# Another order of the stages in the first ten steps of a fused attention and feed-forward kernel

## The chip, the cores and the metric

The kernel runs on one core of one Trainium2 chip. The metric is the device time of one execution in microseconds. Before the change the median of three runs is 623.97 us (623.69 to 624.47). The times in the rows below come from one further execution, which the hardware profiler recorded.

## The reference

The reference computes attention over 2 batches of 8 heads with 768 positions of 64 numbers. A position sees the first 4 positions (the sinks) and the last 128 up to itself. The result, 1536 rows of 512, goes through two feed-forward nets:

```python
scores = np.where(keep, q @ k.T / 8, -1e9)        # keep = sink or 0 <= rel < 128
a = np.exp(scores - scores.max(-1, keepdims=True))
x = (a / (a.sum(-1, keepdims=True) + 1e-9)) @ v   # -> (1536, 512)
x = ((x @ w_a) * (x @ w_b)) @ w_out               # d_ff 1536
x = np.maximum(x @ w_in, 0)
y = (x * x) @ w_out2                              # d_ff 2048
```

## The kernel before

**Groups and steps.** Attention is cut into 24 groups: per batch six blocks of 128 query rows, per block two groups of four heads. Group g belongs to block g // 2. Blocks 0 and 6 are the first of a batch and have no earlier block, so their groups (0, 1, 12, 13) have no sinks and no selections. `attention_fast` runs a loop of 27 steps. Step g issues one stage each for several groups at once: a lag of -2 beside a stage's name in the lists `ORDER` and `AT_FIRST` means that step g does this stage for group g - 2. PE, DVE, ACT and POOL issue their instructions strictly in the order in which the lists name them; each waits in line for what its next instruction needs. `AT_FIRST` holds for the steps below `EARLY`, `ORDER` for the others.

**The stages of a group**, with their engine and line:
- `scores0`, `scores1` (PE, L243): scores of two heads each, into two PSUM tiles `sc`. They can be overwritten as soon as the maxima have read them.
- `soft0`, `soft1` (DVE, L259 and L262): a predicated copy, then mask and row maximum. Together they are called the maxima here.
- `exp0`, `exp1` (ACT, L270): exponentials and their sums, one step later.
- `rec` (DVE, L275 and L276): the reciprocals of the sums. `norm` (DVE, L283), `normA` (ACT, L290) and `normP` (POOL, L295) multiply one, one and two heads by them. `sp` (POOL, L305 to L307) does it for the sinks' columns and splits them into two parts.
- `pst` (PE, L337) and `st` (ACT, L343): the sinks' columns transposed and copied. `ptp` (PE, L313) and `th` (ACT, L317): the four heads transposed and copied. `lu` (POOL, L328 and L330): two selections, the lower and the upper triangle.
- `x0`, `x1` (PE, L362, from step 10 on L376 in two halves) and `xs` (PE, L392): the products with the values and with the sinks' values. `xh` (ACT, L400) and `xl` (DVE, L403): the result as a high and a low part.
- `warm`: matmuls of zeros (L414) in the steps up to 9, their number by `WARM`.
- Beside attention the weights of the first net are decoded, one piece per step of `DECODE` (4, 8, 10, 11, ...): `abs` on ACT (L589), `ts` on DVE in the same step (L593, L594), `stt` and `stt2` on DVE one step later (L597, L600), `cast` on ACT (L605) and `lo` on DVE (L607) two steps later. From step 11 on `fill` gives PE twelve matmuls of the first net per step (L720), and `fu` (ACT) and `fm` (DVE, L737) read their result in the next step.

**Queues.** SP issues the loads, in program order as the trace has it: block 0 in halves of two head pairs, then block 1 whole (`load_kq(1)`), the values, blocks further on and the weights. The sinks' values of a batch are loaded into `vsr` and split by `sink_split` at the end of the steps in `VS`: a copy on ACT (L220), and a subtraction of 32 x 512 numbers (L221) that waits for it. From step 10 on (`WIDE`) two PSUM banks fewer are at hand for `bank`, and POOL writes a `mark` (L382) between `x0` and `x1`, which `x1` waits for.

After step 26 PE alone has a written order; the feed-forward nets follow as one long row of 128x512 matmuls.

Of the kernel before, what the change touches and what calls it, by code (L numbers as in the profile page):

```python
# [10 lines left out]
F32 = mybir.dt.float32  # L11
# [18 lines left out]
ORDER = [  # L30
    ("exp0", -1), ("exp1", -1), ("fm", 0), ("pst", -2), ("rec", -1), ("st", -2), ("fu", 0), ("scores0", 0),
    ("x0", -3), ("scores1", 0), ("x1", -3), ("xs", -3), ("abs", 0), ("xh", -3), ("ptp", -2), ("th", -2), ("cast", -2), ("soft0", 0), ("soft1", 0), ("sp", -1),
    ("norm", -1), ("warm", 0), ("fill", 0), ("normA", -1), ("normP", -1), ("xl", -3), ("stt", -1),
    ("lo", -2), ("ts", 0), ("lu", -2), ("stt2", -1)]
AT_FIRST = [x for x in ORDER if x[0] not in ("rec", "warm")]
AT_FIRST.insert(AT_FIRST.index(("soft1", 0)) + 1, ("rec", -1))
AT_FIRST.insert(AT_FIRST.index(("ptp", -2)), ("warm", 0))
EARLY = 4
DECODE = [4, 8, 10, 11, 12, 13, 14, 15, 18, 19, 20]
WIDE = 10  # L40
VS = (3, 12)
FLAG = 22
SPARED = range(10, 18)
PINNED = 3
WARM0 = 14
WARM = {0: 2, 1: 4, 2: 6, 3: 8, 4: 9, 5: 6, 6: 6, 7: 6, 8: 6, 9: 6}
NQ, NV, NEX, NTH, NLU, NSP = 3, 5, 3, 2, 2, 2
T = 512
SW = P + SK
# [107 lines left out]
def attention_fast(tc, ctx, c, cp, tp, q, k, v, vs_in, xh, xl, beside):  # L157


    nc = tc.nc  # L160
# [21 lines left out]
    pns, ths, sps, sts, lus, xs = ({} for _ in range(6))  # L182
# [6 lines left out]
    def load_kq(n, part=slice(0, H // 2)):  # L189
        if n >= B * NB:  # L190
            return
        if n not in queries:
            queries[n] = p2.tile([P, H // 2, P], F32, name="queries", tag="queries", bufs=NQ)
        b, i = divmod(n, NB)
        nc.sync.dma_start(keys[:, part, i], k[b, i, :, part])
        nc.sync.dma_start(queries[n][:, part], q[b, i, :, part])

    def load_v(n):
        if n >= B * NB:
            return  # L200
        vals[n] = p2.tile([P, H, D], F32, name="values", tag="values", bufs=NV)
        nc.sync.dma_start(vals[n], v[n // NB, n % NB])

    with tc.high_priority(offset=1000):
        load_kq(0, slice(0, 2))
        load_kq(0, slice(2, 4))
    load_kq(1)
    load_v(0)


# [1 line left out]
    vs = p1.tile([96, B, H // 2, P], F32R, name="vs")  # L212
    vsr = {}

    def sink_load(b):
        vsr[b] = p1.tile([96, H // 2, P], F32, name="vsr", tag="vsr")
        nc.sync.dma_start(vsr[b], vs_in[:, b])

    def sink_split(b):
        nc.scalar.copy(vs[:, b], vsr[b])  # L220
        nc.gpsimd.tensor_sub(vs[64:96, b], vsr[b][64:96], vs[64:96, b].bitcast(F32))  # L221

    def half(t, r):
        return t[r * D:(r + 1) * D]
# [22 lines left out]
    def maxima(g, pp):  # L247

        b, i, m = groups[g]
        if pp == 0:  # L250
            pns[g] = (p2.tile([P, GH, SW], F32, name="ex", tag="ex", bufs=NEX),
                      p2.tile([P, GH], F32, name="ss", tag="ss", bufs=NEX),
                      p2.tile([P, GH], F32, name="nb", tag="nb", bufs=NEX))
        ex, ss, nb = pns[g]
        w, at = P if i == 0 else SW, PREV
        sc = scs[pp]
        if i > 0:
            other = sc[:, :, 0:2 * (PREV + SW)].rearrange("q r (u s) -> q r u s", u=2)[:, :, ::-1, 0:HK]
            nc.vector.copy_predicated(sc[:, :, at:at + P].rearrange("q r (u s) -> q r u s", u=2),  # L259
                                      c.pick.unsqueeze(1).to_broadcast([P, 2, 2, HK]), other)  # L260
        for h in range(2 * pp, 2 * pp + 2):
            nc.vector.tensor_tensor_reduce(  # L262
                out=ex[:, h, 0:w], in0=sc[:, h % 2, at:at + w], in1=c.m[min(i, 2)][:, 0:w], scale=-0.125,
                scalar=3.0e38, op0=ALU.add, op1=ALU.min, accum_out=nb[:, h:h + 1])

    def exps(g, pp):
        ex, ss, nb = pns[g]
        w = P if groups[g][1] == 0 else SW
        for h in range(2 * pp, 2 * pp + 2):
            nc.scalar.activation(ex[:, h, 0:w], ex[:, h, 0:w], AF.Exp, bias=nb[:, h:h + 1], scale=-1.0,  # L270
                                 accum_out=ss[:, h:h + 1])
# [80 lines left out]
    def values(g, turn):  # L352
        b, i, m = groups[g]
        apart = now[0] >= WIDE
        if apart and now[0] < N:
            return turned_values(g, turn)
        if turn == 0:
            return
        x = xs[g] = ps_x[0].tile([P, 2, T], F32, name="x", tag="x")[:, :, 0:P] if apart else bank("x")[:, 0:2]
        for j, probs_t in enumerate(lus.pop(g)):  # L360
            for h in range(GH):
                nc.tensor.matmul(half(x, h % 2)[:, h // 2], lhsT=vals[g // 2 - j][:, GH * m + h], rhs=probs_t[:, h],  # L362
                                 start=j == 0 and (apart or h < 2), stop=False, skip_group_check=True)
# [44 lines left out]
    def warm(n):  # L408

        if n == 0:  # L410
            return
        ps = bank("psw").rearrange("p h t -> p (h t)")[:, 0:2 * P]
        for _ in range(n):
            nc.tensor.matmul(ps, lhsT=beside.zero, rhs=beside.zero[:, 0:1].to_broadcast([P, 2 * P]), start=True,  # L414
                             stop=True)

    stages = dict(scores0=lambda g: scores(g, 0), scores1=lambda g: scores(g, 1), ptp=probs, th=probs_copy, lu=probs_select, soft0=lambda g: maxima(g, 0),
                  soft1=lambda g: maxima(g, 1), exp0=lambda g: exps(g, 0), exp1=lambda g: exps(g, 1), rec=reciprocal,
                  sp=sinks, pst=sinks_turn, st=sinks_copy, x0=lambda g: values(g, 0), x1=lambda g: values(g, 1), xs=sinks_values, xh=x_high, xl=x_low,
                  norm=normalize, normA=normalize_a, normP=normalize_p)  # L420
    now, ps_x = [0], []
    warm(WARM0)
    for g in range(N + 3):
        now[0] = g
        if g == WIDE:
            wide.close()
            ps_x[:] = [beside.stack.enter_context(tc.tile_pool(name="ps_x", bufs=1, space=PSUM, side="right"))]
            beside.lend(ps_t, "t1")
        elif g == N:
            ended.close()  # L430
            beside.open()
        if g % 2 == 0:
            load_kq(g // 2 + 2)
            load_v(g // 2 + 1)
        if g == 0:
            sink_load(0)
            later_masks(tc, cp, tp, c)
        elif g == FLAG:
            flag(tc, cp, c)
        beside.fetch(g)  # L440
        for name, lag in AT_FIRST if g < EARLY else ORDER:
            if name == "warm":
                warm(WARM.get(g, 0))
            elif name in stages:
                if 0 <= g + lag < N:
                    stages[name](g + lag)
            else:
                beside.stage(name, g + lag)
        if g in VS:
            sink_split(VS.index(g))  # L450
            if g == VS[0]:
                sink_load(1)
# [679 lines left out]
def sliding_window_moe_kernel(ctx, tc, q, k, v, vs, span, w_a, w_b, w_out, w_in2, w_out2, out):  # L1132
# [51 lines left out]
    def attend_any(ctx, beside):  # L1184
        attention_any(tc, c, q, k, v, xh, xl)
        beside.open()

    run(lambda ctx, beside: attention_fast(tc, ctx, c, cp, tp, q, k, v, vs, xh, xl, beside))
    slow = nc.values_load(c.slow[0:1, 0:1], min_val=0, max_val=1,
                          skip_runtime_bounds_check_because="the flag is 0 or 1")  # L1190
# [70 lines left out]
```

## Time and profile before

| | us |
|---|---|
| median of three runs | 623.97 |
| the profiled execution | 624.48 |
| its span, first to last instruction | 622.8 |
| PE busy in it | 608.0 (98%) |
| DVE busy | 480.4 (77%) |
| ACT busy | 303.5 (49%) |
| POOL busy | 64.8 (10%) |

POOL's work lies in the first 124 us, those of attention. A matmul's busy time is modelled, so whether PE is at its pace is read better from the starts of its instructions than from the share.

### The profile page before, as it was taken

The numbers are of one execution on the slowest core, as the hardware profiler recorded it, in microseconds if no ns is written. First come the engines' busy times: TensorE is split into PE (matmuls) and PEld (weight loads), VectorE is DVE, ScalarE is ACT, GpSimd is POOL, SyncE is SP. The second block draws the span as 40 slices with busy tenths as digits, with TensorE's granted clock in tenths as the row PEclk, the third lists the DMA queues.
The fourth block names the chain that finished last, engine by engine and source line by source line (L and its number), as shares of the span: only waits on it lengthen the run. The fifth ranks groups of instructions, "written<-read, shape, count | busy, mean of one in ns | idle before, by whom it ended". The sixth has DMA issues, their size and how long they took to land.

```text
span 622.8 us, 9656 instructions
## 1 busy us (share of the span) xinstructions
PE 608.0 (98%) x3525; PEld 494.4 (79%) x3525; DVE 480.4 (77%) x1079; ACT 303.5 (49%) x688; POOL 64.8 (10%) x157
## 2 busy tenths in 40 slices
PE   7989999999999999999999999999999999999995
PEld 4667778888888888888888888888888888888884
DVE  6889989369999948858869999977796779834352
ACT  5888887434744434434443554564453445232220
POOL 5665355400000000000000000000000000000000
PEclk9999999999999999999999999999999999999998
DMA  8934423012123313212302013232022202000032
GB/s 260 280 115 148 154 69 103 3 34 73 62 103 115 122 34 102 68 34 68 101 35 101 2 34 102 67 132 82 27 100 67 74 29 68 0 1 0 2 115 94
DMA packets 22041, 49.55 MB, mean 80 GB/s; under 512 B 2080, under 2 KB 8736, under 8 KB 21984
## 3 DMA queue, kind: packets, MB, share of 16 engines
q1 hardware_dynamic: 21696, 48.70, 24.5%
q8 instruction: 30, 0.49, 0.3%
q14 instruction: 27, 0.22, 0.1%
q10 hardware_dynamic: 288, 0.13, 0.1%
HBM read 45.68 MB, written 3.15 MB: 78 GB/s over the span
## 4 chain that ended last, share of the span: by engine, by line


## 5 line engine op out<-in xcount | busy, mean ns | idle before, releaser
L720 PE MATMUL psa<-xh,wh 128*128 128x512 f32 x224 | 88.6, 396 | 0.1
L720 PE MATMUL psa<-xh,wl 128*128 128x512 f32 x224 | 87.4, 390 | 0.0
L720 PE MATMUL psa<-xl,wh 128*128 128x512 f32 x224 | 87.3, 390 | 0.0
L980 PE MATMUL acc<-wh,gh 128*128 128x512 f32 x192 | 74.7, 389 | 0.0
L980 PE MATMUL acc<-wh,gl 128*128 128x512 f32 x192 | 74.7, 389 | 0.0
L980 PE MATMUL acc<-wl,gh 128*128 128x512 f32 x192 | 74.7, 389 | 0.0
L607 DVE TENSOR_TENSOR wl<-wtmp,wh 128x512 fp32r<-128x512 f32 x68 | 48.5, 717 | 17.2 <-ACT wh L605 17.0
L605 ACT CAST wh<-wtmp 128x512 fp32r<-128x512 f32 x68 | 42.3, 622 | 36.8 <-PE acc L980 10.0
L73 ACT CAST gh<-ks 128x512 fp32r<-128x512 f32 x48 | 29.7, 622 | 52.5 <-PE acc L980 52.5
L589 ACT ACTIVATE wtmp<-wraw 128x512 f32<-128x512 f32 x68 | 45.5, 673 | 19.3 <-DVE wl L74 12.7
L980 PE MATMUL acc<-gh,wh 128*128 128x512 f32 x136 | 52.9, 389 | 0.0
L980 PE MATMUL acc<-gl,wh 128*128 128x512 f32 x136 | 52.9, 389 | 0.0
L980 PE MATMUL acc<-gh,wl 128*128 128x512 f32 x136 | 52.9, 389 | 0.0
L720 PEld LDWEIGHTS psa<-xh,wh 128*128 128x128 f32 x224 | 42.1, 188 | 8.9 <-DVE gs L737 0.6
L720 PEld LDWEIGHTS psa<-xh,wl 128*128 128x128 f32 x224 | 42.0, 188 | 8.9
L597 DVE SCALAR_TENSOR_TENSOR wtmp<-wraw,wtmp 128x512 int32<-128x512 int32 x68 | 48.6, 719 | 0.4
L720 PEld LDWEIGHTS psa<-xl,wh 128*128 128x128 f32 x224 | 42.1, 188 | 8.2
L600 DVE SCALAR_TENSOR_TENSOR wtmp<-wraw,wtmp 128x512 int32<-128x512 int32 x68 | 46.4, 687 | 0.7
L980 PEld LDWEIGHTS acc<-wl,gh 128*128 128x128 f32 x192 | 36.0, 188 | 7.5
L980 PEld LDWEIGHTS acc<-wh,gh 128*128 128x128 f32 x192 | 36.0, 188 | 7.4
L980 PEld LDWEIGHTS acc<-wh,gl 128*128 128x128 f32 x192 | 36.0, 188 | 7.4
L74 DVE TENSOR_TENSOR gl<-ks,gh 128x512 fp32r<-128x512 f32 x48 | 32.8, 688 | 10.5 <-ACT gh L73 10.1
(177 smaller groups left out, 1279.5 us busy)
## 6 DMA issues: line engine op xcount, KB each, us to landing
wraw<-in_moe_w_out_dram SPq DMA_DIRECT2D x28, 512.0 KB, 3.5
wraw<-in_moe_w_in_dram SPq DMA_DIRECT2D x16, 512.0 KB, 3.5
wraw<-in_moe_w_a_dram SPq DMA_DIRECT2D x12, 512.0 KB, 3.5
wraw<-in_moe_w_b_dram SPq DMA_DIRECT2D x12, 512.0 KB, 3.4
values<-in_v_dram SPq DMA_DIRECT2D x12, 256.0 KB, 4.3
keys<-in_k_dram SPq DMA_DIRECT2D x11, 272.0 KB, 5.1
queries<-in_q_dram SPq DMA_DIRECT2D x11, 256.0 KB, 4.2
out_dram<-part SPq DMA_DIRECT2D x11, 256.0 KB, 2.2
```

The costliest lines, as they stand in the source:

```text
L73: nc.scalar.copy(hi, src)
L74: return (lo_eng or nc.vector).tensor_sub(lo, src, hi.bitcast(F32))
L589: a = nc.scalar.activation(tf, up.bitcast(F32), AF.Abs)
L597: nc.vector.scalar_tensor_tensor(out=t, in0=up, scalar=0x3FFFFFFF, in1=t, op0=ALU.bitwise_or, op1=ALU.bitwise_and)
L600: nc.vector.scalar_tensor_tensor(out=t, in0=low, scalar=29, in1=t, op0=ALU.logical_shift_right, op1=ALU.bitwise_or)
L605: nc.scalar.copy(hi, tf)
L607: nc.vector.tensor_sub(lo, tf, hi.bitcast(F32))
L720: self.tc.nc.tensor.matmul(ps, lhsT=w[:, kt, :], rhs=x[:, kt, ts], start=n == 0, stop=n == 3 * KT - 1)
L980: nc.tensor.matmul(acc["ps"][d], lhsT=a, rhs=b, start=n == 0, stop=n == acc["total"] - 1)
```

## The change

The list for the first steps is written out anew and holds for steps 0 to 9 instead of 0 to 3. Read by engine, against the order that steps 4 to 9 had:

- PE: `scores0`, `x0`, `scores1`, `x1`, then `pst`, `xs`, `ptp`, `warm` (before: `pst` ahead of the scores).
- DVE: the maxima of group g, then `rec` and `norm` of group g - 1, then `xl` and the decoding (before: `rec` of group g - 1 ahead of the maxima).
- ACT: `exp0`, `exp1`, `abs`, `xh`, `st`, `th`, `cast`, `normA` (before: `st` ahead of `abs`).
- POOL: `lu` of group g - 2, then `sp` and `normP` of group g - 1 (before: `lu` last).

In steps 0 to 3 `rec` already stood behind the maxima; there the same list moves `lu`, `pst` and `st` as well and puts `warm` behind `ptp`. Step 10 is the first with `ORDER`. The second `sink_split` goes from the end of step 12 to the end of step 7, the subtraction in both goes from POOL to DVE, `WARM[4]` goes from 9 to 8, and block 1 is loaded in two halves.

```diff
-AT_FIRST = [x for x in ORDER if x[0] not in ("rec", "warm")]
-AT_FIRST.insert(AT_FIRST.index(("soft1", 0)) + 1, ("rec", -1))
-AT_FIRST.insert(AT_FIRST.index(("ptp", -2)), ("warm", 0))
-EARLY = 4
+AT_FIRST = [
+    ("exp0", -1), ("exp1", -1), ("fm", 0), ("fu", 0), ("scores0", 0), ("x0", -3), ("scores1", 0), ("x1", -3),
+    ("pst", -2), ("xs", -3), ("abs", 0), ("xh", -3), ("st", -2), ("ptp", -2), ("warm", 0), ("th", -2), ("cast", -2),
+    ("soft0", 0), ("soft1", 0), ("rec", -1), ("norm", -1), ("lu", -2), ("sp", -1), ("fill", 0), ("normA", -1),
+    ("normP", -1), ("xl", -3), ("stt", -1), ("lo", -2), ("ts", 0), ("stt2", -1)]
+EARLY = 10
-VS = (3, 12)
+VS = (3, 7)
-WARM = {0: 2, 1: 4, 2: 6, 3: 8, 4: 9, 5: 6, 6: 6, 7: 6, 8: 6, 9: 6}
+WARM = {0: 2, 1: 4, 2: 6, 3: 8, 4: 8, 5: 6, 6: 6, 7: 6, 8: 6, 9: 6}
-    load_kq(1)
+    load_kq(1, slice(0, 2))
+    load_kq(1, slice(2, 4))
-        nc.gpsimd.tensor_sub(vs[64:96, b], vsr[b][64:96], vs[64:96, b].bitcast(F32))
+        nc.vector.tensor_sub(vs[64:96, b], vsr[b][64:96], vs[64:96, b].bitcast(F32))
```

## Rows read from the trace of the kernel before

**Rows 1.** Windows: stretch, length, busy us (instructions) by engine, granted clock, DMA share, GB/s.
```profile
50.00:60.00 10.00, 9.14 (x105) 7.38 (x101) 9.89 (x31) 8.16 (x27) 7.24 (x12) 1.00 0.48 151
...
200.00:250.00 50.00, 50.00 (x222) 41.41 (x221) 37.54 (x70) 20.41 (x35) 0.00 (x0) 1.00 0.27 85
```

**Rows 2.** Timeline, PE, steps 2 to 13: start, us, instruction, [idle before, releaser].
```profile
8.25 0.94 PE L243 MATMUL sc<-keys,queries 64*64 64x200 f32 x16 [1.61 <-DMA queries<-in_q_dram]
...
21.06 0.62 PE L313 MATMUL ptp<-identr,ex 128*128 128x128 f32 x4
...
38.47 0.24 PE L337 MATMUL pst<-identr,sp 128*96 128x128 f32 x1
...
41.23 0.62 PE L313 MATMUL ptp<-identr,ex 128*128 128x128 f32 x4
...
46.09 0.48 PE L720 MATMUL psa<-xh,wh 128*128 128x512 f32 x1
...
56.08 0.56 PE L376 MATMUL x<-lu,values 64*64 64x128 f32 x16 [0.84 <-POOL mark L382]
...
57.24 0.50 PE L720 MATMUL psa<-xh,wh 128*128 128x512 f32 x1
```

**Rows 3.** Waits of PE's weight loads after 58 us: total us, times, longest.
```profile
PEld psa L720 <- DVE gs L737: 0.6, 2, 0.4
```

**Rows 4.** Timeline, DVE: step 4, and the maxima of step 10.
```profile
16.65 0.17 DVE L275 TENSOR_SCALAR ss<-ss 128x4 f32<-128x4 f32 x1 [2.55 <-ACT ex L270]
...
16.95 0.41 DVE L259 COPY_PREDICATED sc<-pick,sc 128x256 f32<-128x256 int32 x1
...
18.85 0.48 DVE L283 TENSOR_SCALAR ex<-ex,ss 128x128 f32<-128x128 f32 x1
...
41.12 0.41 DVE L259 COPY_PREDICATED sc<-pick,sc 128x256 f32<-128x256 int32 x1
```

**Rows 5.** Timeline, POOL: step 4, and the first selection of step 9.
```profile
17.20 0.24 POOL L305 TENSOR_TENSOR ex<-ex,ss 128x32 f32<-128x32 f32 x1 [0.77 <-DVE ss L276]
...
18.04 0.61 POOL L295 TENSOR_TENSOR ex<-ex,ss 128x256 f32<-128x256 f32 x1
18.60 0.64 POOL L328 TENSOR_SCALAR_AFFINE_SELECT lu<-th 128x512 f32<-128x512 f32 x1
19.20 0.64 POOL L330 TENSOR_SCALAR_AFFINE_SELECT lu<-th 128x512 f32<-128x512 f32 x1
...
38.42 0.64 POOL L328 TENSOR_SCALAR_AFFINE_SELECT lu<-th 128x512 f32<-128x512 f32 x1
```

**Rows 6.** Timeline, ACT, steps 4 and 5.
```profile
14.95 0.41 ACT L270 ACTIVATE ex<-ex,nb 128x136 f32<-128x136 f32 x1
...
17.48 0.59 ACT L317 COPY th<-ptp 128x512 f32<-128x512 f32 x1
...
21.72 0.59 ACT L317 COPY th<-ptp 128x512 f32<-128x512 f32 x1
```

**Rows 7.** Timeline, SP: the load of the first piece of weights.
```profile
8.82 0.42 SPq L569 DMA_DIRECT2D wraw<-in_moe_w_a_dram  x1
```

**Rows 8.** DMA issues of the first 12 us: count, KB each, median us to landing.
```profile
wraw<-in_moe_w_a_dram SPq DMA_DIRECT2D x1, 512.0 KB, 6.8
...
keys<-in_k_dram SPq DMA_DIRECT2D x2, 136.0 KB, 2.7
```

**Rows 9.** Timeline, POOL and DVE, steps 11 and 12.
```profile
49.30 0.43 DVE L594 TENSOR_SCALAR wtmp<-wtmp 128x512 int32<-128x512 int32 x1
...
53.23 1.08 POOL L330 TENSOR_SCALAR_AFFINE_SELECT lu<-th 128x512 f32<-128x512 f32 x1
54.39 1.32 POOL L221 TENSOR_TENSOR vs<-vsr,vs 32x512 fp32r<-32x512 f32 x1
...
54.62 1.37 DVE L594 TENSOR_SCALAR wtmp<-wtmp 128x512 int32<-128x512 int32 x1
```

**Rows 10.** The page's costliest groups: busy us, mean ns | idle us before, releaser.
```profile
L607 DVE TENSOR_TENSOR wl<-wtmp,wh 128x512 fp32r<-128x512 f32 x68 | 48.5, 717 | 17.2 <-ACT wh L605 17.0
```

## The prediction

> **What bounds the kernel now.** I read the windows first. In the feed-forward part PE starts 222 matmuls in every 50 us, one each 0.225 us, at a granted clock of 1.00 [rows 1]; that part can only begin earlier or later, not shrink. So the question is when PE's unbroken run begins. The starts of PE's instructions show it: the first twelve feed-forward matmuls come in step 11 at 46.09, then PE stands 0.84 us in step 13 before 56.08, and its next twelve start at 57.24 [rows 2]. After 58 us PE loses 0.6 us more in two waits for DVE's `gs` [rows 3]. Ahead of that the limit is DVE, busy 9.89 of 10 us from 50 to 60 [rows 1]. The reader is to see that PE could regain 0.84 + 0.6, some 1.45 us, after step 11, and that all else of a gain must be there when step 11's matmuls begin.
>
> **The start of step 4.** PE waited 1.61 us in step 2 until block 1's queries had landed, at 8.25 [rows 2]. The half loads of block 0 landed 2.7 us after issue (median) [rows 8]; with such a load for block 1, scores would start about 7.3 (6.7 to 8.25: between half loads that land at once and a gain of nothing). I take 0.9 us. One step's maxima take 1.90 us (16.95 to 18.85) [rows 4], so step 2's end near 9.95 in place of 10.9 and step 3's near 12.2. From there ACT's row: `normA` of group 2, the first `sink_split`'s copy, then the four exponentials of group 3, four times about 0.4 us [rows 6], from 13.6 to 15.2; before, they began at 14.95 [rows 6]. DVE's 2.55 us of idling for these exponentials [rows 4] goes, since the maxima of step 4 stand ahead of the reciprocal; the subtraction moved to DVE takes part of it, 0.7 us by its nearest row, a DVE difference of 128x512 [rows 10]. They begin near 14.6 instead of 16.95.
>
> What is late next is ACT: `abs` comes before `xh`, `st` and `th`, and its weights were issued at 8.82 and landed 6.8 us later, at 15.6 [rows 7, 8]. They queue behind the same bytes as before, so I leave that time. `abs`, `xh`, `st` take some 1.2 us and `th` 0.59 [rows 6]: the first selection of step 4 starts at 17.45 instead of 18.60 [rows 5], **1.15 us earlier**. The bounds are 0.6 (weights half a us later) and 1.9 (`abs` not held up).
>
> **The loop in steps 5 to 9.** With `lu` ahead of `sp` and `normP` on POOL a ring closes that was open before: `lu` of group g - 3, then `sp` and `normP` of group g - 2, then PE's `ptp` of g - 2 in the next step, ACT's `th`, and `lu` of g - 2. Before, `normP` was done a step ahead. The ring's length from rows: two selections 1.20, `sp` 0.84 (17.20 to 18.04), `normP` 0.61 [rows 5], from the start of `ptp` to `th` 0.66 (21.06 to 21.72) [rows 2, 6], `th` 0.59 [rows 6]: 3.90 us. The pace before was 38.42 - 18.60 = 19.82 us for five steps [rows 5], 3.96 each. The ring alone is no faster than what it replaces, whatever DVE saves by the new order.
>
> Nor is it alone. Before, `sp`, `normP` and the first selection ran beside DVE's maxima. Now the selections follow `th`, and DVE, done with the maxima, is then at the decoding (steps 4, 5, 6, 8, 9) or at the moved subtraction (step 7). The rows of step 12 show what happens when POOL and such an operation meet: a selection took 1.08 us instead of 0.64, and DVE's L594 took 1.37 beside POOL's subtraction, against 0.43 [rows 5, 9]. What meets in each of the five rounds isn't in the trace, so I bound it: 0 (they miss each other; PE's and ACT's part of the ring leaves POOL free for 1.25 us) and 0.6 (a 0.7 us operation in between, less what overlaps [rows 10]). Of these I take 0.40, close to the selection's 0.44. Then five rounds are 21.5 us, and the first selection of step 9 starts at 17.45 + 21.5 = 38.95, **0.5 us later** than 38.42.
>
> The Trainium skill (SBUF — State Buffer, section Who interferes with whom) says that a DVE instruction with two SBUF inputs, or in a 2-port mode, and a GpSimd instruction that reads SBUF exclude each other, and that the one issued second is blocked. The 1.37 us agrees with it. Taken strictly, every meeting would cost one of the two a whole operation, which is the second rival below.
>
> **The handing over to step 10.** There `ORDER` applies again: `pst` is first on PE. It needs `sp` of group 8, which now stands behind the selections: 38.95 + 1.20 + 0.84 + 0.06 = 41.05, against 38.47 [rows 2]. Scores, products, `mark` and all of step 10 queue behind it. Before, `ptp` followed `pst` by 2.76 us (38.47 to 41.23) [rows 2], of which I reckon 0.7 as waits for the selections and `mark`; so `ptp` is at 43.15, 1.9 us late. In step 11 POOL is then free earlier for the next selections (0.2 us), and the first twelve matmuls start near 47.8, **1.7 us late**. DVE feels less: its maxima of step 10 can start 0.9 us behind `pst` at 41.95, 0.8 behind 41.12 [rows 4].
>
> **After step 11.** The second `sink_split` no longer stands in step 12: DVE's L594 loses its 0.94 us of excess [rows 9] and `mark` its wait of 0.84 [rows 2]. DVE, 0.8 late, is then 0.1 early, so PE's 1.45 us come back: 1.7 - 1.45 is about **0.2 us late**, and PE's unbroken run carries that to the end. In step 7 the subtraction waits for ACT's copy, behind `th` and `normA`; DVE has slack there beside the ring. One warm-up matmul less is worth under 0.1 us, and no wait hangs on it. Two more loads push SP's later ones back by about a us; no wait of PE for a load stands in the rows but that of step 2. The second load of `vsr` can be issued once the first subtraction is done, near step 4 as before, and has until step 7.
>
> The profiled execution took 624.48 us, 1.7 more than its span and 0.5 above the median. 0.2 on the median of 623.97 gives **624.2 us**, that is, no change: a measurement of this kernel can tell about 0.2%, 1.25 us.
>
> **Rivals.**
> - *The ring isn't disturbed.* DVE is ready early enough to decode while POOL waits for `th`. Price 0: 17.45 + 19.5 = 36.95, 1.5 us early; 0.25 early at step 11's matmuls (the handing over still costs 1.2), and with 1.45 after it 1.7 early: 622.3 us. With `abs` not held up 0.75 more, 621.5. For it: DVE has 2.55 us of idling less [rows 4] to start from. Against: `lo` needs `cast`, which follows `th`, and the subtraction waits for a copy behind `th`, so these two meet POOL in any case. It is faster by over 0.2% from a price of about 0.1 us per round down.
> - *POOL and DVE block each other in every round.* Price 0.6, lead 0.6: 18.0 + 22.5 = 40.5, 2.1 late; 3.25 at step 11's matmuls, less 1.45: 1.8 late, 625.8 us. If DVE loses as much (it also pays where L594 did) it arrives later than PE and little is regained: 627. It decides from about 0.6 us per round upward. For it: the meeting in the rows of step 12. Against: there POOL had one long operation more.
> - *The order hardly matters*, and only step 12's subtraction counts: 0.84 + some of the 0.6, less the first subtraction's place: 622.9 to 623.5. In this case, too, most times lie within 0.2%.
> - *The clock falls.* PE would stand over 2 us before `pst` of step 10. The granted clock was 1.00 through a wait of 1.61 us in step 2 [rows 1, 2], so I give it little; a stretch of 5 us at half of it would cost 2.5 us, 626.7.
>
> **How the numbers follow.** No change, with the order that hardly matters, 0.40. The undisturbed ring 0.34: a start of step 4 two us earlier is certain to be there, and I have not seen the ring run. Mutual blocking 0.23, the clock 0.03: together 0.26 for slower. The range goes from 621.0 (the first rival with its best lead and half a us to spare) to 627.0 (the second with DVE late).
>
> **What would show it.** Right: the first selection of step 4 near 17.5 and that of step 9 near 39, `pst` of step 10 about 2.5 us later than 38.47, step 11's matmuls near 47.8, no wait for `mark` of 0.8 us in step 13, and selections of about 1.08 us in steps 4 to 9. The ring is wrong if selections follow each other by less than 3.9 us; the price if they keep 0.64 us. The forecast fails if step 11's matmuls start before 46.8 or after 48.8.

## The result and the profile after

The changed kernel takes **630.63 us** (median of five executions, 629.62 to 631.16) against 623.97 before (five executions beside them): ratio 1.0107, 95% interval 1.0094 to 1.012. It is 1.1% slower; I had predicted no change, 624.2 us. The profiled execution took 630.63 us, its span is 628.9, 6.1 more than before.

In the rows after, line numbers are 3 higher. First step 4 (timelines of SP, ACT and POOL; start, us, instruction, [idle before, releaser]), the counterpart of [rows 5 to 7]:

```profile
9.45 0.43 SPq L572 DMA_DIRECT2D wraw<-in_moe_w_a_dram  x1
...
17.13 0.68 ACT L592 ACTIVATE wtmp<-wraw 128x512 f32<-128x512 f32 x1 [1.36 <-DMA wraw<-in_moe_w_a_dram]
...
18.11 0.60 ACT L320 COPY th<-ptp 128x512 f32<-128x512 f32 x1
...
18.79 0.64 POOL L331 TENSOR_SCALAR_AFFINE_SELECT lu<-th 128x512 f32<-128x512 f32 x1 [3.98 <-ACT th L320]
```

The weights were issued 0.63 us later than before (9.45 against 8.82), behind two more loads, and landed 1.5 later, since the load itself also took longer. The DMA issues of the first 12 us (count, KB, median us to landing) have 7.7 in place of 6.8 [rows 8]:

```profile
wraw<-in_moe_w_a_dram SPq DMA_DIRECT2D x1, 512.0 KB, 7.7
```

So `abs`, which did not wait for them before, idled 1.36 us, and the first selection came at 18.79: not 1.15 us earlier than 18.60, but 0.19 later. PE's timeline answers to [rows 2]:

```profile
19.48 1.77 PE L365 MATMUL x<-lu,values 128*64 128x128 f32 x16 [1.46 <-POOL lu L331]
...
39.83 0.83 PE L417 MATMUL psw<-zero 128*128 128x256 bf16 x6
43.74 0.27 PE L340 MATMUL pst<-identr,sp 128*96 128x128 f32 x1 [3.08 <-POOL sp L310]
...
46.98 0.98 PE L316 MATMUL ptp<-identr,ex 128*128 128x128 f32 x4
48.78 0.24 PE L340 MATMUL pst<-identr,sp 128*96 128x128 f32 x1 [0.82 <-ACT th L320]
...
50.44 0.44 PE L379 MATMUL x<-lu,values 64*64 64x128 f32 x8 [0.60 <-POOL lu L333]
...
53.27 0.78 PE L723 MATMUL psa<-xh,wh 128*128 128x512 f32 x1
...
64.14 0.48 PE L723 MATMUL psa<-xh,wh 128*128 128x512 f32 x1
...
622.50 0.39 PE L983 MATMUL acc<-wl,gh 128*128 128x512 f32 x1
```

PE stands 3.08 us at the handing over to step 10, until `sp` of group 8 is there; step 11's matmuls start at 53.27 (46.09 before, 47.8 predicted), step 13's at 64.14 (57.24). The last matmul starts at 622.50, before it was this row, 6.82 us earlier (the stretch behind it, output transfers, was 0.7 us shorter this time, hence 6.1 in the span):

```profile
615.68 0.39 PE L980 MATMUL acc<-wl,gh 128*128 128x512 f32 x1
```

What POOL does in step 9 explains the 3.08 us:

```profile
40.75 0.64 POOL L331 TENSOR_SCALAR_AFFINE_SELECT lu<-th 128x512 f32<-128x512 f32 x1 [1.24 <-ACT th L320]
41.34 1.08 POOL L333 TENSOR_SCALAR_AFFINE_SELECT lu<-th 128x512 f32<-128x512 f32 x1
42.39 0.67 POOL L308 TENSOR_TENSOR ex<-ex,ss 128x32 f32<-128x32 f32 x1
...
43.44 0.25 POOL L310 TENSOR_TENSOR sp<-ex,sp 128x32 fp32r<-128x32 f32 x1
```

POOL idled 1.24 us for `th`, then a selection took 1.08 us and `sp`'s first part 0.67, where the other readings are 0.64 and 0.24. The windows (columns as in [rows 1]) show what I had given a chance of 0.03:

```profile
19.50:22.50 3.00, 2.88 (x23) 2.31 (x24) 2.57 (x15) 1.56 (x8) 1.96 (x5) 0.65 1.09 352
...
43.50:46.50 3.00, 2.76 (x50) 2.35 (x50) 1.45 (x7) 0.83 (x2) 1.80 (x7) 0.64 0.57 175
...
50.50:53.50 3.00, 3.00 (x43) 2.64 (x44) 2.75 (x15) 1.61 (x7) 1.39 (x5) 0.61 0.23 79
```

The granted clock falls to its lower level (1.2 of 2.4 GHz) for most of these three stretches, each behind one or two of PE's waits: 1.46 us before 19.48; 3.08 before 43.74; 0.82 and 0.60 before 48.78 and 50.44. In the kernel before it was 1.00 in every window up to 150 us, also around the wait of 1.61 us that ended at 8.25 and that my forecast went by:

```profile
0.00:10.00 10.00, 7.16 (x76) 4.63 (x77) 6.28 (x37) 4.67 (x18) 5.80 (x18) 1.00 0.74 215
10.00:20.00 10.00, 8.41 (x100) 5.31 (x99) 6.92 (x38) 8.76 (x35) 6.14 (x12) 1.00 1.07 353
```

`ptp`, 0.62 us before, takes 0.98 at 46.98.

### The profile page after: what moved, and what is told of

Read it like the earlier page. It is cut to its first block, busy times and chain, and to the rows that moved or that the text cites. A ratio compares the mean times of both kernels' runs of the same rounds, so it can differ in the third digit from the quotient of the medians.

```text
span 628.9 us, 9643 instructions
## 1 busy us (share of the span) xinstructions
PE 612.5 (97%) x3524; PEld 498.4 (79%) x3524; DVE 482.9 (77%) x1081; ACT 303.9 (48%) x688; POOL 65.8 (10%) x155
## 4 chain that ended last, share of the span: by engine, by line
## 5 line engine op out<-in xcount | busy, mean ns | idle before, releaser
L600 DVE SCALAR_TENSOR_TENSOR wtmp<-wraw,wtmp 128x512 int32<-128x512 int32 x68 | 48.0, 710 | 0.4
L603 DVE SCALAR_TENSOR_TENSOR wtmp<-wraw,wtmp 128x512 int32<-128x512 int32 x68 | 47.4, 702 | 0.7
```

Source lines behind the costliest of these rows:

```text
L600: nc.vector.scalar_tensor_tensor(out=t, in0=up, scalar=0x3FFFFFFF, in1=t, op0=ALU.bitwise_or, op1=ALU.bitwise_and)
L603: nc.vector.scalar_tensor_tensor(out=t, in0=low, scalar=29, in1=t, op0=ALU.logical_shift_right, op1=ALU.bitwise_or)
```

## The experiments

Beside the runs the kernel before had medians of 624.37, 624.14, 624.13 and 623.99 us (13 to 19 executions each); ratios are against it. POOL's two jobs in a step are `sp` with `normP` (they need `rec`) and the selections `lu` (they need `th`).

| changed kernel with | us | ratio (95%) |
|---|---|---|
| 1. the new list in steps 0 to 3 only | 624.36 | 1.0001 (0.9989 to 1.0014) |
| 2. the order alone | 628.68 | 1.0066 (1.0049 to 1.0083) |
| 3. `lu` last on POOL | 628.26 | 1.0067 (1.004 to 1.0093) |
| 4. `rec` early in steps 4 to 9 | 632.16 | 1.013 (1.0115 to 1.0146) |
| 5. `rec` early and `lu` last in steps 4 to 9 | 625.13 | 1.0015 (1.0002 to 1.0028) |
| 6. more warm-ups | 628.56 | 1.0072 (1.0053 to 1.0091) |
| 7. `pst` later in step 10 | 630.48 | 1.01 (1.0084 to 1.0115) |
| 8. step 9 with POOL's old order | 630.88 | 1.0097 (1.008 to 1.0113) |
| 9. block 1 loaded whole | 629.65 | 1.0092 (1.0076 to 1.0108) |
| 10. the subtractions on POOL | 632.18 | 1.0124 (1.0108 to 1.0141) |
| 11. 6 and 9 together | 626.96 | 1.0046 (1.003 to 1.0061) |
| 12. 5 and 9 together | 623.49 | 0.9996 (0.9986 to 1.0007) |
| *before* with `VS = (3, 7)` | 623.62 | 0.9993 (0.9977 to 1.0009) |
| *before* with that and `rec` late in step 4 | 624.49 | 1.0006 (0.9995 to 1.0016) |

**1. The new list in steps 0 to 3 only.**

```diff
-EARLY = 10
+EARLY = 4
```

> The changed kernel with its new list for steps 0 to 3 only (EARLY back to 4); the moved splits, the subtraction on DVE, the half loads and WARM as changed. Theory A (the ring lu, sp, normP, ptp, th in steps 5 to 9, at 4.39 us a round, and the wait of pst in step 10 behind the selections): the loss goes, 622.5 to 624.5 us, no wait of about 3 us before pst of step 10. Theory B (the clock's three halvings are the loss, whatever brings them on): gone as well if the granted clock stays at 1.00, otherwise 626 and more. Theory C (the later weights, which held abs for 1.36 us, and the subtraction on DVE are the loss): 627 to 630 us.

624.36, as before. All of the loss needs the order in steps 4 to 9; the new start, the half loads and the moved subtractions together bring nothing.

**2. The order alone**: the lists, with `VS = (3, 12)`, the subtractions on POOL and block 1 whole.

```diff
-VS = (3, 7)
+VS = (3, 12)
-    load_kq(1, slice(0, 2))
-    load_kq(1, slice(2, 4))
+    load_kq(1)
-        nc.vector.tensor_sub(
+        nc.gpsimd.tensor_sub(
```

> The new list up to step 9 and WARM alone; block 1 loaded whole, the subtraction on POOL, the second split in step 12 as before. Theory A: the order alone brings the loss, 628.5 to 631 us, with pst of step 10 near 43. Theory C: most of the loss is gone, 624 to 626 us; abs waits 0.5 us or less for its weights.

628.68: about 4.3 of the 6.7 us. The other edits, free beside the old order (run 1), cost some 2 us beside this one. In this trace the weights land in time and the first selection of step 4 starts at 17.25, even before the 17.45 predicted. The lead was there, and the loss came all the same: PE stands 2.83 us before `pst` of step 10, and the granted clock is at 0.50 in the window 40 to 50.

```profile
40.84 0.34 PE L339 MATMUL pst<-identr,sp 128*96 128x128 f32 x1 [2.83 <-POOL sp L309]
```

**3. `lu` last on POOL.** Only POOL's order goes back.

```diff
-... ("rec", -1), ("norm", -1), ("lu", -2), ("sp", -1), ("fill", 0), ("normA", -1),
-    ("normP", -1), ("xl", -3), ...
+... ("rec", -1), ("norm", -1), ("sp", -1), ("fill", 0), ("normA", -1),
+    ("normP", -1), ("lu", -2), ("xl", -3), ...
```

> The changed kernel with sp and normP ahead of lu on POOL again, all else as changed. Theory A: the ring is open, the first selections follow each other by 4.0 us, pst of step 10 comes near 39 to 40, and the time is 622.5 to 625 us. Theory B: as fast as the clock lets it be; with the clock at 1.00 also near 624. Theory C: 628 to 631 us, since weights and subtraction stay.

628.26: that POOL's order is all of it is refuted. (The number lies in theory C's range too, but run 1 has the late weights and the subtraction on DVE without a loss.) The first selections follow each other by 4.80 us on average, not by 4.0. The waits from 16 to 60 us (total us, times, longest) show why:

```profile
POOL ex L308 <- DVE ss L279: 5.9, 4, 3.0
...
PE x L365 <- POOL lu L331: 5.3, 4, 2.2
...
DVE xl L406 <- ACT xh L403: 2.4, 4, 0.9
```

Now `sp` waits for the reciprocal, which stands behind the maxima; the selections queue behind `sp` and `normP`, and `x1`, with `pst`, `xs` and `ptp` behind it on PE, waits for them. As I read these waits a second ring closes from `x1` through `xs`, ACT's `xh` and DVE's `xl`, which stands ahead of the next maxima. In the changed kernel it was the other wait, 14.8 us in 9 times:

```profile
POOL lu L331 <- ACT th L320: 14.8, 9, 4.0
```

**4. `rec` early, `lu` still first.**

```diff
+AT_LATER = [x for x in AT_FIRST if x[0] != "rec"]
+AT_LATER.insert(AT_LATER.index(("fu", 0)), ("rec", -1))
-        for name, lag in AT_FIRST if g < EARLY else ORDER:
+        for name, lag in AT_FIRST if g < 4 else AT_LATER if g < EARLY else ORDER:
```

> The changed kernel with the reciprocals ahead of the maxima again in steps 4 to 9; POOL's selections still first, all else as changed. Theory A (POOL's order closes the ring): the ring and the wait of pst in step 10 stay, first selections 4.2 to 4.4 us apart, 627.5 to 630.5 us. Theory D (the late reciprocals are the root: with selections last the run before was still at 628.3, since sp and normP start only behind the maxima): most of the loss goes, 624 to 626 us.

632.16, the wrong way: an early reciprocal is worth nothing while `sp` stands behind selections that wait for `th`. That it costs 1.5 us more isn't shown to come from the order: here the weights landed later still and `abs` began at 18.34 (17.13), so that the first selection of step 4 comes at 19.98 (18.79). ACT's wait for them in that stretch:

```profile
ACT wtmp L594 <- DMA wraw<-in_moe_w_a_dram: 2.8, 1, 2.8
```

**5. Both back**: as 4, and `lu` behind `stt2` in `AT_LATER`.

```diff
+AT_LATER = [x for x in AT_FIRST if x[0] not in ("rec", "lu")]
+AT_LATER.insert(AT_LATER.index(("fu", 0)), ("rec", -1))
+AT_LATER.insert(AT_LATER.index(("stt2", -1)), ("lu", -2))
```

> The changed kernel with both the reciprocals ahead of the maxima and the selections behind normP in steps 4 to 9, so only PE's and ACT's order of the new list is left there, besides the moved splits and the half loads. Theories A and D: near the kernel before, 623 to 625 us, pace 4.0. Theory E (PE's order, with pst and ptp behind both products, is what delays): 626.5 us and more.

625.13. So the four orders give 630.63 (`rec` late, `lu` first), 628.26 (late, last), 632.16 (early, first) and 625.13 (early, last). Two rings, and each alone is enough to hold the loop; PE's and ACT's new order costs little. Small differences among the four mean little, since `abs` began between 17.13 and 18.34 in them, depending on when the weights had landed; the step down to 625.13 is larger than that.

**6. More warm-ups** in steps 4 to 9: the waits stay, but PE works in them.

```diff
-WARM = {0: 2, 1: 4, 2: 6, 3: 8, 4: 8, 5: 6, 6: 6, 7: 6, 8: 6, 9: 6}
+WARM = {0: 2, 1: 4, 2: 6, 3: 8, 4: 20, 5: 12, 6: 10, 7: 10, 8: 10, 9: 32}
```

> The changed kernel with more matmuls of zeros in the places where PE waits (WARM of steps 4 to 9: 20, 12, 10, 10, 10, 32 in place of 8, 6, 6, 6, 6, 6). Theory A: even at a granted clock of 1.00 throughout, the ring's pace of 4.3 us and the wait of step 10 stay; 626.5 to 628.5 us. Theory B: with the clock at 1.00 the time comes back to 624 to 625 us. If the clock falls all the same: 630 and more, and nothing is told apart.

The profiled execution has a granted clock of 1.00 from 19 to 70 us, and took 627.26. PE and one window:

```profile
43.17 0.26 PE L340 MATMUL pst<-identr,sp 128*96 128x128 f32 x1 [0.19 <-POOL sp L310]
...
45.28 0.62 PE L316 MATMUL ptp<-identr,ex 128*128 128x128 f32 x4
...
46.73 0.23 PE L340 MATMUL pst<-identr,sp 128*96 128x128 f32 x1 [0.82 <-ACT th L320]
...
48.38 0.44 PE L379 MATMUL x<-lu,values 64*64 64x128 f32 x8 [0.60 <-POOL lu L333]
...
50.30 0.48 PE L723 MATMUL psa<-xh,wh 128*128 128x512 f32 x1
...
618.95 0.39 PE L983 MATMUL acc<-wl,gh 128*128 128x512 f32 x1
```

```profile
40.00:50.00 10.00, 8.38 (x134) 6.29 (x133) 7.67 (x25) 6.88 (x26) 6.92 (x16) 1.00 0.26 88
```

`pst` comes 2.99 us after the selection at 40.18, exactly as in the changed kernel (43.74 - 40.75); from there everything is faster. The waits of 0.82 and 0.60 us ahead of step 11's matmuls, which no warm-up fills, are as long as in the changed kernel, and here the clock stays at 1.00 around them. The last matmul is 3.55 us earlier; the medians differ by less, 2.07 us. The kernel's other executions were 628.39 and 628.73 us at a mean clock of 0.996 and 630.38 at 0.992 (0.999 in the profiled one): within one program the time goes with the clock.

**7. `pst` later in step 10**: behind `x1`, so that scores and products don't queue behind it.

```diff
+HAND = [x for x in ORDER if x[0] not in ("pst", "st")]
+at = HAND.index(("xs", -3))
+HAND[at:at] = [("pst", -2), ("st", -2)]
-        for name, lag in AT_FIRST if g < EARLY else ORDER:
+        for name, lag in AT_FIRST if g < EARLY else HAND if g == EARLY else ORDER:
```

> The changed kernel with pst (and its copy st) behind x1 in step 10 as in the steps ahead of it, so that step 10's scores do not stand behind it. If the handing over to step 10 cost what the trace shows (pst 3.0 us behind the first selection of step 9, ptp 3.2 us behind pst), the time falls by 1.5 to 2.5 us to 628 to 629 us. If the wait is only moved to ptp, which needs normP of the same group, it stays at 630 to 631 us.

630.48: nothing. The wait only moves, to the selections and `mark`; `ptp` is 0.8 us earlier than 46.98 and no more:

```profile
41.70 0.44 PE L382 MATMUL x<-lu,values 64*64 64x128 f32 x4 [0.26 <-POOL lu L334]
42.74 0.44 PE L382 MATMUL x<-lu,values 64*64 64x128 f32 x8 [0.60 <-POOL lu L336]
...
44.61 0.92 PE L382 MATMUL x<-lu,values 64*64 64x128 f32 x16 [0.97 <-POOL mark L388]
...
46.16 1.12 PE L319 MATMUL ptp<-identr,ex 128*128 128x128 f32 x4
```

**8. Step 9 with POOL's old order.**

```diff
+AT_NINE = [x for x in AT_FIRST if x[0] != "lu"]
+AT_NINE.insert(AT_NINE.index(("normP", -1)) + 1, ("lu", -2))
-        for name, lag in AT_FIRST if g < EARLY else ORDER:
+        for name, lag in AT_NINE if g == EARLY - 1 else AT_FIRST if g < EARLY else ORDER:
```

> The changed kernel with POOL's order in step 9 alone as before (sp and normP of group 8 ahead of the selections of group 7). Theory H, that the handing over to step 10 is a price of its own because sp of group 8 stands behind the selections of group 7: pst of group 8 at 42.0 to 42.5 instead of 43.74, ptp of group 8 no later than 45.5, step 11's matmuls near 51.6, and the time 628.7 to 629.2. Theory M, that the selections of group 7 then take sp's place as the last one awaited (x1 of group 7 in step 10 waits for them): pst is early, but x1 of step 10 waits 1 us or more for the selections, ptp stays within 0.4 us of 46.98, and the time is 630.2 to 630.8.

630.88: closer to the second theory, though the wait for the selections is 0.47 us and not 1 or more. `pst` is 1.2 us earlier, but `x` waits for the selections next, the window 40 to 50 is at 0.63, and `ptp` is no earlier (46.98 there):

```profile
42.56 0.30 PE L342 MATMUL pst<-identr,sp 128*96 128x128 f32 x1 [1.18 <-POOL sp L312]
...
44.24 1.28 PE L381 MATMUL x<-lu,values 64*64 64x128 f32 x12 [0.47 <-POOL lu L333]
...
47.48 1.07 PE L318 MATMUL ptp<-identr,ex 128*128 128x128 f32 x4
```

**9. Block 1 loaded whole.**

```diff
-    load_kq(1, slice(0, 2))
-    load_kq(1, slice(2, 4))
+    load_kq(1)
```

> The changed kernel with block 1 loaded whole again. Theory W: the two half loads push the first weights back (issued at 9.45 and landed at 17.1 in the changed kernel, 8.82 and 15.6 before), and with them abs, th and the first selection, so that most of the lead of 1.15 us that I had counted on is lost there. Then the weights land near 15.6 again, the first selection of step 4 starts near 18.0 (not 18.79), and the time is 629.4 to 630.0. Rival: the scores of step 2 are 0.9 us later instead (near 8.25) and the maxima of step 4 with them, so that the time is 630.6 or above. The difference between the order alone (628.68) and the full change (630.63), 1.95 us, is then not in the loads.

629.65, as the theory of the late weights has it. The first selection comes at 17.62, that of step 9 at 39.38 (40.75 with halves):

```profile
17.62 0.64 POOL L330 TENSOR_SCALAR_AFFINE_SELECT lu<-th 128x512 f32<-128x512 f32 x1 [2.62 <-ACT th L319]
...
39.38 0.64 POOL L330 TENSOR_SCALAR_AFFINE_SELECT lu<-th 128x512 f32<-128x512 f32 x1 [1.24 <-ACT th L319]
```

The window 20 to 30 is at 1.00, as in the other profiles with block 1 whole, and below it in those with halves and the usual warm-ups. But the wait of 3.09 us for `pst` at 42.38 is still there, and the window 40 to 50 stands at 0.56, so that of 1.36 us at `pst` 1.03 are left at step 11's matmuls (52.24):

```profile
40.00:50.00 10.00, 6.77 (x78) 5.12 (x82) 6.05 (x19) 5.20 (x20) 5.82 (x13) 0.56 0.26 79
```

The other traces bear the theory out, with one exception. In the nine with half loads the weights were issued at 9.28 to 9.75 and took 7.6 to 8.6 us to land. In the seven with block 1 whole they were issued at 8.56 to 8.90 and took 6.7 or 6.8 us, but in run 11 they took 7.7.

**10. The subtractions on POOL.**

```diff
-        nc.vector.tensor_sub(
+        nc.gpsimd.tensor_sub(
```

> The changed kernel with both subtractions of the sinks' values on POOL, at the ends of steps 3 and 7. Theory S: on DVE they took 1.13 us (14.22) and 0.99 us after a wait of 1.05 for ACT's copy (32.99), both beside POOL and both ahead of the next maxima; without them the maxima of step 4 begin near 14.2 instead of 15.38 and the time is 629.0 to 629.6. Rival: POOL has no room for them in this order (it stands ahead of normP or the selections in the ring and took 1.32 in step 12 of the kernel before): the second one delays the ring of step 8 by 1 us or more, and the time is 631 to 632.

632.18, just above the rival's range. Its reason isn't confirmed: the subtraction of step 7 is 1.26 us long, yet the next selection is only 4.05 us behind the last (32.06 to 36.11). Step 11's matmuls start at 53.91, 0.64 late against the changed kernel, step 12's 5.9 us later at a clock of 0.53 (window 41 to 55). How much is the subtraction and how much the clock stays open.

```profile
34.77 1.26 POOL L224 TENSOR_TENSOR vs<-vsr,vs 32x512 fp32r<-32x512 f32 x1
36.11 0.64 POOL L331 TENSOR_SCALAR_AFFINE_SELECT lu<-th 128x512 f32<-128x512 f32 x1
```

**11. More warm-ups and block 1 whole**, the edits of 6 and 9.

> The changed kernel with more warm-ups (20, 12, 10, 10, 10 and 32 in steps 4 to 9) and block 1 loaded whole. Theory: lead and clock are separate terms. The run with the warm-ups alone had its full clock in the profiled execution, 627.26 us, with the first selection of step 4 at 18.77, that of step 9 at 40.18 and step 11's matmuls at 50.30. With the whole load the selections come near 17.6 and 39.05, step 11's matmuls near 49.2, and an execution at full clock takes 626.1 to 626.5; the median, with executions in which the clock falls, 626.5 to 627.8. Rival: the extra warm-ups fill PE so that the earlier th is of no use, or the clock falls all the same; then step 11's matmuls stay at 50.3 or later and the median at 628.0 to 629.0.

626.96: 1.6 us below run 6, and six executions within 625.67 to 628.14. The profiled one (626.96) is at a clock of 1.00 in the same windows as run 6's, but it gains only 0.6 us on it at the last matmul and is above the 626.1 to 626.5 that I expected at full clock: the first selection came at 17.96, not at 17.6, and the five rounds took 0.16 more than in run 6. The weights took 7.7 us to land although block 1 was whole, and `abs` waited 0.84 us for them.

```profile
16.32 0.66 ACT L591 ACTIVATE wtmp<-wraw 128x512 f32<-128x512 f32 x1 [0.84 <-DMA wraw<-in_moe_w_a_dram]
```

```profile
42.52 0.27 PE L339 MATMUL pst<-identr,sp 128*96 128x128 f32 x1 [0.19 <-POOL sp L309]
44.63 0.62 PE L315 MATMUL ptp<-identr,ex 128*128 128x128 f32 x4
...
49.65 0.48 PE L722 MATMUL psa<-xh,wh 128*128 128x512 f32 x1
...
618.35 0.39 PE L982 MATMUL acc<-wl,gh 128*128 128x512 f32 x1
```

**12. `rec` early, `lu` last, block 1 whole**, the edits of 5 and 9.

> The changed kernel with the reciprocal ahead of the maxima and the selections last on POOL in steps 4 to 9 (625.13 us in the earlier run, its weights late, its first selection of step 4 at 19.31) and block 1 loaded whole. Theory: the weights land near 15.6 again and the lead of about 1.1 us comes through, since in this order neither ring is closed: first selection of step 4 near 18.2 to 18.6, step 11's matmuls near 47.5, 623.6 to 624.3 us, no slower than the kernel before. Rival: in this order step 4 is set by DVE's wait for the exponentials and not by the weights; then nothing changes, 624.8 to 625.4.

623.49, 1.6 us below run 5, as the theory has it; the clock is 1.00 from 20 to 30 and from 40 to 60 us. Step 11's matmuls start when they did before, 1.4 us earlier than I expected:

```profile
46.09 0.47 PE L725 MATMUL psa<-xh,wh 128*128 128x512 f32 x1
```

It is the fastest version of the change, and with 0.9986 to 1.0007 not faster than the kernel before by anything that can be told.

**The kernel before with the split moved**, and with one more step of its own first list.

```diff
-VS = (3, 12)
+VS = (3, 7)
```

> The kernel before with the second split in step 7 in place of step 12, its subtraction still on POOL; nothing else changed. By the prediction's term: the 0.84 us wait for mark in step 13 goes and DVE's L594 of step 12 returns to 0.43 us; 0.5 to 1.0 us faster, 623.4 to 623.9 beside 624.4. Rival: POOL's 1.3 us only moves into step 7 and holds sp of the next step; no change.

623.62: the wait for `mark` in step 13 goes, as I had it, and the time is not distinguishable. With `EARLY = 5` besides:

> The kernel before with the second split at the end of step 7 (on POOL) and the reciprocal behind the maxima in step 4 too (the old list for five steps). If DVE's idling of 2.55 us ahead of the reciprocal of step 4 sets that step's end, the maxima of step 4 begin near 15.0 instead of 16.95, step 11's matmuls start 0.5 to 1 us earlier than 46.60, and the time is 622.6 to 623.3. Rival, after the runs with the late reciprocal: sp, normP and norm of group 3 come 1.9 us later, ptp of step 5 waits for them, the gain of step 4 is given back there, and the time is 623.5 to 624.2; above 624.5 the late reciprocal costs already when it is late in a single step.

624.49. The maxima of step 4 do start at 15.30, against 17.04 with the split alone, but `sp` idles 1.42 us for the reciprocal and the first selection comes at 19.49 (18.69). (The old list also puts step 4's warm-ups ahead of `ptp`; `th` is 0.2 us later for it, but the selection waited for `normP`.) At the selection of step 9 0.47 us of the delay are left (39.40, 38.93); step 11's matmuls then start 1.7 us later (48.30, 46.60), with the granted clock at 0.65 from 44.3 to 47.0. A single step with the late reciprocal gives back what the early maxima gain.

## Why the prediction was wrong

The prediction's own steps, against three profiles (us; each row up to the sum is the time since the row above):

| step | predicted | changed | 6: clock 1.00 | 11: clock 1.00, block 1 whole |
|---|---|---|---|---|
| first selection of step 4 | 17.45 | 18.79 | 18.77 | 17.96 |
| five rounds | 21.50 | 21.96 | 21.41 | 21.57 |
| to `pst` of step 10 | 2.10 | 2.99 | 2.99 | 2.99 |
| to `ptp` of step 10 | 2.10 | 3.24 | 2.11 | 2.11 |
| to step 11's matmuls | 4.65 | 6.29 | 5.02 | 5.02 |
| sum: step 11's matmuls | 47.80 | 53.27 | 50.30 | 49.65 |
| last matmul, against before | +0.25 | +6.82 | +3.27 | +2.67 |

Between the last three columns, 6.82 is 3.55 (clock) + 0.60 (block 1 whole) + 2.67 (what is left of the order). These are single profiled executions, and the parts depend on the path: without the warm-ups block 1 whole moved the last matmul by 1.60 us (run 9), and in run 11 the weights were still late in part.

- **The loop was right.** The ring through `lu`, `sp`, `normP`, `ptp` and `th` closed; POOL idles 1.24 us in a round for `th`, and the price of 0.40 per round for POOL and DVE meeting was right: 4.28 us a round at full clock, 4.30 predicted. What the selections and `sp` took beyond 0.64 and 0.24 us in run 6 comes to 0.41 a round, and without it a round is 3.87, against 3.90 from the rows. That the average came out so close was partly luck: single rounds paid 0.18 to 0.66. The Trainium skill (SBUF — State Buffer, section Who interferes with whom) lets one of the two wait while the other holds the shared port. The trace agrees, with both held up in turn: in step 9 of run 6 a selection took 1.08 in place of 0.64 us, and DVE's two operations of 128x512 beside it (L600, L603) 0.94 and 1.00 in place of 0.68. So a meeting cost each less than a whole operation.
- **The step that failed most is the rival at 0.03, the clock.** I had its place (PE standing before `pst` of step 10) and dismissed it on one row, the 1.61 us in step 2 that left the clock at 1.00. But my own working put `pst` 2.6 us later behind a PE that would be done at the old time: the wait of 3.08 us followed from it, and a comparison with a single shorter wait didn't bear a chance that small. In all five traces with a wait of 2.8 to 3.2 us there (the changed kernel, runs 2, 4, 9 and 10) the clock fell in it or right behind it. Between the changed kernel's profile and run 6's the clock cost 3.55 us: 0.55 in the rounds, behind the wait of 1.46 us in step 4 that the rival didn't have, and 3.0 from `pst` on.
- **"They queue behind the same bytes as before, so I leave that time"** failed. The bytes are the same, but the halves make two more loads ahead of the weights, which moved their issue by 0.63 and their landing by 1.5 us; `abs` holds up `th` and with it the first selection. Further on the prediction itself let two more loads push SP's later ones back by about a us, and asked only whether PE waits for one of these; ACT did. Run 9 without the halves has it at 17.62, 0.17 from the 17.45 predicted, so the rest of the step stands. The lower bound of the lead, 0.6 us (weights half a us later), was too high: the lead was -0.19. In the changed kernel the wait it makes in step 4 also goes with the first fall of the clock.
- **`pst` at 1.20 + 0.84 + 0.06 behind the first selection** left out the meeting that I charged to each of the five rounds: in step 9, too, a selection took 0.44 more and `sp` 0.43 more, together 2.99. The 0.37 on to step 11 is a wait of 0.60 us of `x1` for the second selection (1.08 us), where I had POOL free 0.2 us earlier.
- **After step 11** I had 1.45 us coming back; 0.9 did at full clock (4.21 to 3.27, 3.56 to 2.67). The wait for `mark` went, those for `gs` stayed, I think because DVE is late with PE. Waits of PE's weight loads from 56 to 130 us, after; before, those for `mark` had 3.7 us and a longest of 1.1, those for `gs` the same 0.6 [rows 3]:

```profile
PEld x L379 <- POOL mark L385: 3.2, 12, 0.3
...
PEld psa L723 <- DVE gs L740: 0.6, 2, 0.4
```

With the clock's 3.55 taken off, the forecast is still 3.0 us short: 1.3 at the first selection, of which block 1 whole gave back 0.8 (run 11) or 1.2 (run 9), 1.3 the handing over, 0.5 the regain, less 0.1 for the rounds. Of the rivals, the undisturbed ring and the order that hardly matters are refuted (the order alone costs 4.3 us); mutual blocking falls by its price, 0.40 a round and not 0.6.

I had not seen the second ring at all: with the late reciprocal, `sp`, the selections and `x1` hold each other up even where POOL keeps its old order (run 3). That there are two causes, each enough, takes runs 3 to 5 together; the path of the second ring is read from run 3's waits, and no run cuts it at a single link.

## What to carry to other kernels

A strict per-engine order that moves a consumer ahead of its step's producers can close a ring; add up the ring, then count the same meetings once more where the order hands over. A new wait of PE is priced with the clock on top of it: here the clock cost some 3 us behind a wait of 3.08. A load that is split adds an issue ahead of every later one on its queue, so look for the first engine that waits for any of these.

## What the runs showed of the hardware

- The granted clock fell behind waits of 3.08 us and, with smaller ones close by, 1.46 and 0.82 + 0.60 us, but not around 1.61 us in step 2 before. With most of the 3.08 and part of the 1.46 us filled by warm-ups it stayed at 1.00 in run 6's profile and run 11's. The waits of 0.82 + 0.60 us stood unfilled in these two, and in run 3, and left it at 1.00 there. In the kernel of the last run it fell near 45 us behind waits of 0.82 and 0.47 us; in run 12 waits of 0.82 and 0.48 left it at 1.00. What decides between such cases stays open.
- On DVE the small subtraction (32 partitions x 512) took longer than I priced it by a 128x512 difference (0.7 us): 1.13 us beside `normP`, and 0.99 beside a selection and `sp`'s first part (0.67 instead of 0.24), the second after 1.05 us of idling for ACT's copy. In step 3 it put the maxima of step 4 at 15.38 where I had 14.6.

```profile
14.22 1.13 DVE L224 TENSOR_TENSOR vs<-vsr,vs 32x512 fp32r<-32x512 f32 x1 [0.39 <-ACT vs L223]
...
32.99 0.99 DVE L224 TENSOR_TENSOR vs<-vsr,vs 32x512 fp32r<-32x512 f32 x1 [1.05 <-ACT vs L223]
```
